# Attention and a gated two-layer MLP on one core: the MLP's layers in stretches of four blocks, Mish and Exp in separate phases, scores in four PSUM banks

## The chip, the core and the metric

The kernel runs on one core of a Trainium2 chip. The metric is the device time of one execution in microseconds. TensorE (PE) multiplies, VectorE (DVE) and ScalarE (ACT) do elementwise work, GpSimd (POOL) does a few fills, SyncE (SP) issues all DMAs. Each engine works through its own list of instructions in order; an instruction that waits for a semaphore holds up everything behind it on its engine.

## The reference, cut to what matters

```python
# q, k, v: (8, 8, 576, 64); f: (8, 8, 576); w_in: (512, 2048); w_out: (2048, 512), float32
scores = q @ k.T / 8 + (cum[:, :, :, None] - cum[:, :, None, :])   # cum = cumsum(log(clip(f)))
scores = where(causal, -1e9, scores)
attn = exp(scores - max(scores)); attn = attn / (sum(attn) + 1e-9)
x = (attn @ v), heads side by side                                 # (4608, 512)
h = x @ w_in
out = (h * tanh(softplus(h))) @ w_out                              # Mish, then the second layer
```

Float32 accuracy is kept by splitting each factor into a high and a low float16 part and adding three products.

## The kernel before, in words

**The work.** Attention goes by pairs of heads: 32 pairs, four to a batch element. The MLP goes by chunks of 512 tokens: eight chunks from the eight batch elements, and a ninth from their last 64 tokens each. A chunk needs the attention output of its four pairs, transposed, in the tile `xa`.

**A pair of heads** (from the fifth pair on; `new_st_items`, L1119). Its scores come in six blocks, X0, Y0, Z, W (with a small V), X1, Y1, each of one PSUM bank. For a block PE makes the scores (`b<-st`), DVE adds the mask and takes the row maximum in one custom instruction (`b<-b,mskw`, with its accumulator read `mn`), ACT takes Exp from PSUM into a float32 buffer (`st<-b,mn`; the buffer is one of two in the tile `flat2`, L1116), ACT copies that to float16 (`hb<-st`), DVE makes the low part (`hb<-st,hb`), and a DMA transposes both into `pt`. Two slots of the order later PE multiplies by v (`new_pv_items`, L1213: 30 products of 64 or 65 columns for the first head, 60 with the tail for the second; `b<-vv,pt`), DVE normalises (`rr`, `x`), and the result is split and transposed into `xa`. For a coming pair ACT sums squares (`junk<-qk`, `junk<-v`), and DVE or ACT scale and split q, k and v (`hl`, `vv`). The first four pairs are done in another way, with float32 products against v.

**A block of the MLP** (16 to a chunk). The first layer (`m1_items`, L1348) is 12 products of 512 columns into bank 2 or 3 in turn (`b<-xa,wall`); ACT takes Mish (`me<-b,cinv`), DVE or ACT the high part `gh`, DVE the low part `gl`. The second layer (`m2_items`, L1380) is 12 products of 512 columns into banks 4 to 7 (`b<-gh,wall`, `b<-gl,wall`), which sum over the 16 blocks and are then copied out as `ot`. Before, the second layer of a block follows the first layer two blocks behind (`LAG` in the main loop, L1503 and on), across chunk boundaries too. In the first chunk the weights are being unpacked and split as well (`wall`).

**Banks.** Scores, products with v and small sums take banks 0 and 1 in turn (`bank`, L883). Banks 2 and 3 belong to the first layer.

**Mish and Exp** are in two different tables of ACT. A change between them puts an `ACT_TABLE_LOAD` ahead of the next one.

**The order.** `Program` records all operations with their regions, and `schedule` (L294) makes the order: forward passes (L355) that take on each engine, at its own clock by a table of costs, the ripe operation of lowest rank, and backward passes that make the next ranks; the best of ten is written out. In the forward pass ACT prefers an operation of the table that is loaded, within the bound `TSWAP` of ranks. The recorded order mixes attention items among MLP items of the chunk before by their costs (last loop of `attn_moe`, L1571 and on).

Of the kernel before, what the change touches and what calls it, by code (L numbers as in the profile page):

```python
# [15 lines left out]
F32 = mybir.dt.float32  # L16
# [10 lines left out]
P = 128  # L27
# [30 lines left out]
WN = [int(x) for x in ("1", "2",)]  # L58
NME = 5
NOT = 2  # L60
NGH = 5
SPD = 0
WO0 = 16
LWO = 4
# [77 lines left out]
class Program:  # L142
# [9 lines left out]
    def __init__(self, nc):  # L152
        self.nc = nc
        self.ops = []
        self.banks = []
        self.sets = []
        self.rank = None
        for n in self.NAMES:
            setattr(self, n, Queue(self, n))

# [3 lines left out]
    def choose(self, *ways):  # L164
# [24 lines left out]
        self.ops.append((opts, r, w, key))  # L189
        func = ways[0][0][3].get("func") if ways[0][0][0] == "scalar" and len(ways) == 1 else None  # L190
        self.sets.append("mish" if func == AF.Mish else "exp" if func == AF.Exp else None)

        self.banks.append({
            x.tensor.name for _, _, a, kw in ways[0] for x in list(a) + list(kw.values())
# [27 lines left out]
    def cost(self, eng, method, kw, aps):  # L222
# [10 lines left out]
        if eng == "tensor":  # L233

            rows = int(kw.get("in_", kw.get("rhs")).shape[0])
            half = (int(out.offset) // int(out.ap[0][0]) // 64 + 1) * (int(out.shape[0]) == 64)
            if kw.get("rhs") is not None and kw["rhs"].dtype == F32:
                n = max(4 * n, 4 * int(out.shape[0]))
            return max(n, 64), n * rows / 128.0, half
        if eng == "scalar":  # L240
            if method != "activation":
                return 1283
# [314 lines left out]
def attn_moe(ctx: ExitStack, tc: tile.TileContext, qk, v, f, w_in, w_out, out):  # L557
# [325 lines left out]
    def bank(name, shape=(P, CH), dtype=F32):  # L883

        nonlocal nbank
        nbank += 1
        return psum(banks[nbank % len(banks)], shape, dtype)

    def load_qk(g):
        b, p = divmod(g, NP)  # L890
        t = sp.tile([P, 2, S], F32, name=f"qk{g}", tag="qk32", bufs=NQK)
        nc.sync.dma_start(out=t, in_=qk[b, p])
        st[g]["qk"] = t
# [220 lines left out]


    flat2 = ST1[2].rearrange("p j t s -> p (j t s)").bitcast(F32)  # L1116
    ne = [0]

    def new_st_items(g):  # L1119
# [20 lines left out]

        def place_e():
            ne[0] += 1
            return flat2[:, CH * (ne[0] % 2) : CH * (ne[0] % 2 + 1)]

        def turn(e, name):
            h = sp.tile([P, 2, CH], F16, name=f"h{name}{g}", tag="hb", bufs=NHB)
# [4 lines left out]
            s[name] = t  # L1151

        def x_(j):
            ps = bank(f"sx{j}_{g}")
            scores(ps, j, 3 * P, P, 0, CH)
            highest(ps, 4 * j + 3, mskw)
            e = place_e()
            exp(e, ps, 4 * j + 3)
            turn(e, f"X{j}")

        def y_(j):
            ps = bank(f"sy{j}_{g}")
            scores(ps[:, 0:384], j, 2 * P, P, 0, 384)
            scores(ps[:, 384:512], j, 0, P, 0, P)
            highest(ps[:, 0:384], 4 * j + 2, mskw[:, 128:512])
            highest(ps[:, 384:512], 4 * j, mskb)
            e = place_e()
            exp(e[:, 0:384], ps[:, 0:384], 4 * j + 2)
            exp(e[:, 384:512], ps[:, 384:512], 4 * j)
            turn(e, f"Y{j}")  # L1170

        def z_():
            ps = bank(f"sz_{g}")
            for j in range(2):
                scores(ps[:, 256 * j : 256 * j + 256], j, P, P, 0, 256)
            for j in range(2):
                highest(ps[:, 256 * j : 256 * j + 256], 4 * j + 1, mskw[:, 256:512])
            e = place_e()
            for j in range(2):
                w = slice(256 * j, 256 * j + 256)  # L1180
                exp(e[:, w], ps[:, w], 4 * j + 1)
            turn(e, "Z")

        def w_():
            ps, pv = bank(f"sw_{g}"), bank(f"sv_{g}")
            for o, k in ((pv[:, 0:D], slice(CH, S)), (ps, slice(0, CH))):
                beside(*((
                    o[j * D : (j + 1) * D], q1[0 : KM - 1, j, CH:S], k1[0 : KM - 1, j, k], True, False)
# [311 lines left out]
    def w0(fn):  # L1500
        M.append((fn, 0))

    LAG = 2  # L1503
    steps = [(c, j) for c in range(NCHUNK) for j in range(NF)]
    done = 0
    i = 0
    while done < len(steps):
        if i < len(steps):
            c, j = steps[i]
            if j == 0:  # L1510
                cstart[c] = len(M)
                if c == 1:
                    w0(level_all)
                if c:
                    w0(lambda c=c: scale_chunk2(c))
                if c == B:
                    for b in range(B):
                        w0(lambda b=b: scale_tails(b))
            items = m1_items(c, j)
        else:  # L1520
            items = []
        M.extend(items)
        lag = LAG0 if done < NF else LAG
        n = 0
        while i - done >= lag and n < 2 and done < len(steps):
            x = m2_items(*steps[done])
            M.extend(x)
            done += 1
            n += 1
            if i - done < LAG:  # L1530
                break
        i += 1

    ai = 0

# [35 lines left out]
    for c in range(NCHUNK):  # L1571
# [3 lines left out]
        target = marks[last_pair(c + 1)] if c + 1 < NCHUNK else len(A)  # L1575
        a_from = ai
        acost = sum(60 + x[1] for x in A[a_from:target])
        mcost = sum(x[1] for x in M[m0:m1])
        done_a = done_m = 0.0
        for k in range(m0, m1):  # L1580
            M[k][0]()
            done_m += M[k][1]
            while ai < target and done_a < acost * (done_m / mcost):
                done_a += 60 + A[ai][1]
                run_a(ai + 1)
        run_a(target)
    nc.emit()


# [48 lines left out]
```

## Time and profile before

| | |
|---|---|
| time, three runs | 1054.42 us median (1052.96 to 1054.48) |
| the profiled execution | 1054.26 us, span 1052.5 us |
| mean granted TensorE clock | 0.984 |
| busy, of the span | PE 94%, ACT 74%, DVE 70%, POOL 2% |
| table loads on ACT | 202 and one at the start, 1283 ns each |
| bytes | 48.37 MB read, 12.57 MB written in HBM |

The page of the profile gives busy time by engine, the span in 40 slices, the chain of waits that ended last, and groups of instructions. All recorded operations have line L290, the line that writes them out, so groups are told apart by tile names. A busy time is that of the instructions' spans, which overlap; PE's ends are modelled.

### The profile page before, as it was taken

Reading aid. Unit: us, or ns where it says so; the run is one execution under the profiler, and the core shown is the slowest. Engines: PE = TensorE matmul, PEld = TensorE weight load, DVE = VectorE, ACT = ScalarE, POOL = GpSimd, SP = SyncE. Lnnn points to the kernel's source line nnn. Section 1 sums busy time; section 2 is a strip of 40 time slices with the busy share of each in tenths; the row PEclk is TensorE's granted clock in tenths of the full one; section 3 lists DMA queues with packets and bytes.
Section 4 is the critical chain, followed back from the end, with each engine's and each line's share of the span. In section 5 each row is a group of like instructions: output and inputs, shape, how many; then the busy total and the mean of one; then the engine's idle time right before and its main releaser. Section 6 shows DMA issues by size and latency. Waiting matters only on the chain.

```text
span 1052.5 us, 19788 instructions
## 1 busy us (share of the span) xinstructions
PE 987.3 (94%) x7214; PEld 504.9 (48%) x7214; DVE 733.5 (70%) x2040; ACT 779.1 (74%) x1293; POOL 17.3 (2%) x59
## 2 busy tenths in 40 slices
PE   0599788999999999999999999999999999999998
PEld 0387344544445555554544554455544554444443
DVE  8989899998677787777777767787777653222221
ACT  5457899879799999898889989899989782112111
POOL 5000000000000000000000000000000000000000
PEclk9799988999999999999999999999999999999999
DMA  9888997877756766777566756775656432000001
GB/s 297 282 232 212 219 225 174 184 197 190 167 136 149 173 141 152 136 169 143 135 145 138 162 123 143 170 158 128 139 122 149 66 66 73 1 1 21 21 1 40
DMA packets 266258, 146.80 MB, mean 139 GB/s; under 512 B 233808, under 2 KB 234576, under 8 KB 266160
## 3 DMA queue, kind: packets, MB, share of 16 engines
q1 hardware_dynamic: 266160, 145.54, 59.0%
q8 instruction: 56, 0.92, 0.4%
q14 instruction: 42, 0.34, 0.1%
HBM read 48.37 MB, written 12.57 MB: 58 GB/s over the span
## 4 chain that ended last, share of the span: by engine, by line
PE 65%; DVE 13%; ACT 11%; DMA 7%; issue 3%; SPq 1%; ACTq 0%; DVEq 0%
PE b L290 65%; ACT L290 3%; DMA pt<-hb 3%; DVE b L290 2%; ACT st L290 2%; DVE wall L290 2%; ACT hb L290 2%; DVE hl L290 2%; DVE hb L290 2%; ACT junk L290 1%; DVE gl L290 1%; ACT me L290 1%; DMA wall<-in_w_in_dram 1%; DMA qk<-in_qk_dram 1%; DVE vv L290 1%
## 5 line engine op out<-in xcount | busy, mean ns | idle before, releaser
L290 PEld LDWEIGHTS <-wall 128*128 128x128 f16 x3456 | 331.7, 98 | 399.6 <-issue 22.4
L290 PE MATMUL b<-xa,wall 128*128 128x512 f16 x1728 | 418.1, 382 | 10.3 <-DVE wall L290 4.4
L290 PE MATMUL b<-gh,wall 128*128 128x512 f16 x1152 | 371.8, 380 | 0.1
L290 ACT ACT_TABLE_LOAD x202 | 259.2, 1283 | 6.6 <-DVE mn L290 2.6
L290 PE MATMUL b<-gl,wall 128*128 128x512 f16 x576 | 218.9, 380 | 0.0
L290 ACT ACTIVATE me<-b,cinv 128x512 f32<-128x512 f32 x144 | 98.8, 687 | 139.5 <-PE b L290 138.2
L290 DVE TENSOR_SCALAR gh<-me,gsc 128x512 f16<-128x512 f32 x125 | 60.3, 483 | 143.3 <-ACT me L290 142.6
L290 PE MATMUL b<-st 70*128 70x256 f16 (+11 forms) x888 | 139.0, 295 | 21.9 <-ACT st L290 5.2
L290 DVE TENSOR_TENSOR hb<-st,hb 128x512 f16<-128x512 f32 x168 | 114.3, 688 | 57.0 <-ACT hb L290 56.9
L290 ACT ACTIVATE st<-b,mn 128x512 f32<-128x512 f32 (+3 forms) x252 | 127.0, 541 | 34.4 <-DVE mn L290 29.6
L290 PE MATMUL b<-vv,pt 128*128 128x65 f16 (+5 forms) x2576 | 105.2, 202 | 5.6 <-ACT st L290 2.5
L290 DVE SCALAR_TENSOR_TENSOR gl<-me,gsc,gh 128x512 f16<-128x512 f32 x144 | 107.9, 750 | 3.5 <-ACT gh L290 0.3
L290 ACT ACTIVATE hb<-st 128x512 f16<-128x512 f32 x168 | 103.5, 628 | 6.6 <-DMA pt<-hb 5.5
L290 PEld LDWEIGHTS <-st 70*128 70x128 f16 (+3 forms) x888 | 67.6, 104 | 83.2 <-issue 46.0
L290 DVE CUSTOM_DVE_ANT_0 b<-b,mskw 128x512 f32<-128x512 f32 (+1 forms) x168 | 93.9, 565 | 17.6 <-PE b L290 15.1
L290 PEld LDWEIGHTS <-pt 128*128 128x128 f16 (+1 forms) x2352 | 72.5, 102 | 24.3 <-DMA pt<-hb 6.8
L290 DVE SCALAR_TENSOR_TENSOR hl<-qk,qt,hl 128x576 f16<-128x576 f32 x64 | 50.8, 810 | 0.7 <-ACT hl L290 0.7
L290 ACT ACTIVATE junk<-qk 128x576 bf16<-128x576 f32 x64 | 43.5, 679 | 5.9 <-DMA qk<-in_qk_dram 5.2
L290 DVE SCALAR_TENSOR_TENSOR wall<-wall 128x512 int32<-128x512 int32 x64 | 43.5, 686 | 0.1
L290 DVE DVE_READ_ACCUMULATOR2_ANT mn<- 128x1 f32 x280 | 39.8, 142 | 0.0
L290 DVE CUSTOM_DVE_ANT_0 b<-b,mskb 128x128 f32<-128x128 f32 (+1 forms) x84 | 23.6, 281 | 18.4 <-PE b L290 13.5
L290 ACT ACTIVATE junk<-wall 128x512 bf16<-128x512 f32 x32 | 20.1, 628 | 18.8 <-issue 10.5
(102 smaller groups left out, 605.2 us busy)
## 6 DMA issues: line engine op xcount, KB each, us to landing
st<-hl SPq DMA_DIRECT2D x192, 144.0 KB
qk<-in_qk_dram SPq DMA_DIRECT2D x32, 576.0 KB
v<-in_v_dram SPq DMA_DIRECT2D x32, 288.0 KB
out_dram<-ot SPq DMA_DIRECT2D x36, 256.0 KB
wall<-in_w_in_dram SPq DMA_DIRECT2D x16, 512.0 KB
wall<-in_w_out_dram SPq DMA_DIRECT2D x16, 512.0 KB
pt<-hb SPq DMA_TRANSPOSE x168
part<-ot SPq DMA_DIRECT2D x8, 256.0 KB
```

What stands on the lines that cost most here:

```text
L290: r = getattr(real[eng], method)(*a, **kw)
```

## The change

- **Stretches.** From the second chunk on the MLP no longer runs with the second layer two blocks behind: the first layer of four blocks is recorded, then the second layer of these four (`GJ = 4`), four such stretches to a chunk, with nothing of one chunk over into the next. The first chunk is as before.
- **Phases.** Each first-layer part and each second-layer part of a stretch is a phase with a number. Every Mish and every Exp recorded in a phase is made to depend on all Mish and Exp of the phase before. Attention items are now mixed in only among second-layer items, so that Exp falls into second-layer phases and Mish into first-layer phases.
- **Banks.** In the phases scores take banks 0 to 3 in turn (`score_bank`); products with v stay in banks 0 and 1, the first layer in 2 and 3.
- **Buffers.** Two more float32 buffers for Exp (`more_e`, four in all), six `gh`/`gl` pairs instead of five. The scratch space of the DMA rings is set smaller; no instruction uses it.
- **Costs in the order.** A float32 product against v counts 4 times its columns, not at least 512, and half as much activity.

```diff
-NGH = 5
+NGH = 6
+GJ = 4
+NEX = 2
...
+        if self.sets[-1] and self.phase is not None:
+            n = len(self.sets)
+            w.append((f"phase{self.phase}", 0, 1, n, n + 1))
+            r.append((f"phase{self.phase - 1}", 0, 1, 0, 1 << 30))
...
             if kw.get("rhs") is not None and kw["rhs"].dtype == F32:
-                n = max(4 * n, 4 * int(out.shape[0]))
-            return max(n, 64), n * rows / 128.0, half
+                n, active = 4 * n, 2 * active
+            return max(n, 64), active, half
...
+    def score_bank(name):
+        nonlocal nbank
+        if nc.phase is None:
+            return bank(name)
+        nbank += 1
+        return psum(nbank % 4)
...
-            return flat2[:, CH * (ne[0] % 2) : CH * (ne[0] % 2 + 1)]
+            k = ne[0] % (2 + NEX)
+            if k > 1:
+                return more_e[:, k - 2]
+            return flat2[:, CH * k : CH * (k + 1)]
...
-            ps = bank(f"sx{j}_{g}")
+            ps = score_bank(f"sx{j}_{g}")
...
+        for j0 in range(0, NF, GJ):
+            for items in (m1_items, m2_items):
+                phases += 1
+                for j in range(j0, j0 + GJ):
+                    M.extend(x + (phases,) for x in items(c, j))
...
-        mcost = sum(x[1] for x in M[m0:m1])
+        weigh = [x[1] * (len(x) < 3 or x[2] % 2 == 0) for x in M[m0:m1]]
+        mcost = sum(weigh)
         for k in range(m0, m1):
+            nc.phase = M[k][2] if len(M[k]) > 2 else None
             M[k][0]()
-            done_m += M[k][1]
+            done_m += weigh[k - m0]
```

In the program that comes out ACT has 69 table loads instead of 203, and 995 rows instead of 1106; PE's 7214 products are the same. Up to the 16th Mish, the last of the first chunk, the loads are 19 and were 21. Of the operations that either ACT or DVE may do, ACT now has 30 `gh` (19 before) and 40 `xp` (23 before).

**ACT, third chunk.** First before, around its ninth block. `me` is the result of Mish, `st1`, `e4` that of Exp, `hb` and `hv` their float16 copies, `b0` to `b7` are PSUM banks:

```order
L290 ACT_TABLE_LOAD
L290 ACTIVATE me_0_167<-b2_0_117,cinv3_96 128x512
L290 ACT_TABLE_LOAD
L290 ACTIVATE st1_2_84<-b1_0_115,mn_1_166 128x512
L290 ACTIVATE st1_2_84<-b0_0_124,mn_1_166 128x384
L290 ACTIVATE hb_0_162<-st1_2_84 128x512
L290 ACTIVATE st1_2_84<-b0_0_124,mn_1_166 128x128
L290 ACTIVATE xa2_89<-xb_0_183 64x2x64
L290 ACTIVATE hb_1_163<-st1_2_84 128x512
L290 ACTIVATE xa2_89<-xb_0_183 64x2x64
L290 ACT_TABLE_LOAD
L290 ACTIVATE me_1_170<-b3_0_118,cinv3_96 128x512
```

Now, around the Mish of the 13th to 16th block:

```order
L298 ACTIVATE hb_1_164<-more_e_102 128x512
L298 ACT_TABLE_LOAD
L298 ACTIVATE me_4_180<-b2_0_118,cinv3_96 128x512
L298 ACTIVATE hb_0_163<-more_e_102 128x512
L298 ACTIVATE me_0_168<-b3_0_119,cinv3_96 128x512
L298 ACTIVATE gh_3_178<-me_0_168,gsc3_100 128x512
L298 ACTIVATE hb_1_164<-st1_2_84 128x512
L298 ACTIVATE me_1_171<-b2_0_118,cinv3_96 128x512
L298 ACTIVATE hl_0_109<-qk32_0_104,qt_2_135 128x576
L298 ACTIVATE me_2_174<-b3_0_119,cinv3_96 128x512
L298 ACT_TABLE_LOAD
L298 ACTIVATE st1_2_84<-b1_0_116,mn_0_162 128x512
```

One Mish between two loads has become four; the float16 copies of the last scores stand among them.

**PE, third chunk.** Before, where a block's first layer (bank 3, `xa`) runs among second-layer products (`gh`, `gl`) and scores (`st1`, `st2`):

```order
L290 MATMUL b7_0_127<-gh_2_174,wall_69 128x512
L290 LDWEIGHTS wall_69
L290 MATMUL b3_0_118<-xa0_87,wall_69 128x512
L290 LDWEIGHTS st1_0_82
L290 MATMUL b0_0_124<-st1_0_82 128x256
L290 LDWEIGHTS st2_1_86
L290 MATMUL b0_0_124<-st2_1_86 128x256
L290 LDWEIGHTS st1_0_82
L290 MATMUL b0_0_124<-st1_0_82 128x256
L290 LDWEIGHTS st2_1_86
L290 MATMUL b0_0_124<-st2_1_86 128x256
L290 LDWEIGHTS wall_69
```

Now, from the last second-layer products of a stretch to the first product of the next stretch. The six second-layer products ahead of these rows follow on the two products of block X1, which stand in bank 2:

```order
L298 MATMUL b7_0_128<-gh_1_172,wall_69 128x512
L298 LDWEIGHTS st1_0_82
L298 MATMUL b3_0_119<-st1_0_82 128x384
L298 LDWEIGHTS st2_1_86
L298 MATMUL b3_0_119<-st2_1_86 128x384
L298 LDWEIGHTS st1_0_82
L298 MATMUL b3_0_119<-st1_0_82 128x128
L298 LDWEIGHTS st2_1_86
L298 MATMUL b3_0_119<-st2_1_86 128x128
L298 LDWEIGHTS st1_1_83
L298 MATMUL b1_0_116<-st1_1_83 128x512
L298 LDWEIGHTS st2_0_85
```

Block Y1 now stands in bank 3 and X0 of the next pair in bank 1; the next rows are X0's second product and the first layer in bank 2. Before, no score ever stood in bank 2 or 3 while the MLP ran; now each change from second to first layer takes over banks that scores have held.

**DVE at the same place.** Before, a maximum (`ISA`, with the accumulator read as a second row) stands among the parts of Mish:

```order
L290 TENSOR_TENSOR hb_0_162<-st1_2_84,hb_0_162 128x512
L290 ISA b1_0_115,mn_1_166<-b1_0_115,mskb2_80 128x64
L290 ISA mn_1_166 128x1
L290 ISA b0_0_124,mn_1_166<-b0_0_124,mskw_79,mn_1_166 128x512
L290 ISA mn_1_166 128x1
L290 TENSOR_SCALAR gh_1_171<-me_1_170,gsc3_100 128x512
L290 SCALAR_TENSOR_TENSOR gl_1_172<-me_1_170,gsc3_100,gh_1_171 128x512
```

Now, W (bank 0), X1 (bank 2) and Y1 (bank 3) of the same pair:

```order
L298 ISA b0_0_125,mn_2_189<-b0_0_125,mskw_79,mn_2_189 128x512
L298 ISA mn_2_189 128x1
L298 TENSOR_TENSOR hb_1_164<-st1_2_84,hb_1_164 128x512
L298 ISA b2_0_118,mn_2_189<-b2_0_118,mskw_79 128x512
L298 ISA mn_2_189 128x1
L298 TENSOR_TENSOR hb_0_163<-st1_2_84,hb_0_163 128x512
L298 TENSOR_TENSOR hv_0_165<-e4_1_146,hv_0_165 128x128
L298 ISA b3_0_119,mn_2_189<-b3_0_119,mskw_79 128x384
L298 ISA mn_2_189 128x1
```

The maxima of a pair now stand in one run without `gh` and `gl` between them, with low parts of the earlier blocks (`hb`) among them.

**How the 21 changes from second to first layer look**, from the first chunk's end to the end of the regular part (five chunks): in 6 the first layer begins in the bank that X1 held, as above; in 5 the bank of Y1 is wanted about as soon, behind 5 to 11 first-layer products in the other bank; in 10 the bank that is wanted first held W or V, which PE wrote two blocks earlier. The last four stretches with attention are irregular, and from there on the two chunks that are left have no attention.

More of the change, by code (lines that the diff above doesn't have):

```diff
@@ L157, in __init__ @@
         self.rank = None
+        self.phase = None
         for n in self.NAMES:
@@ L236, in cost @@
             half = (int(out.offset) // int(out.ap[0][0]) // 64 + 1) * (int(out.shape[0]) == 64)
+            active = n * rows / 128.0
             if kw.get("rhs") is not None and kw["rhs"].dtype == F32:
-                n = max(4 * n, 4 * int(out.shape[0]))
-            return max(n, 64), n * rows / 128.0, half
+                n, active = 4 * n, 2 * active
+            return max(n, 64), active, half
         if eng == "scalar":
@@ L1116, in attn_moe @@
     flat2 = ST1[2].rearrange("p j t s -> p (j t s)").bitcast(F32)
+    more_e = cp.tile([P, NEX, CH], F32, name="more_e")
     ne = [0]
@@ L1161, in y_ @@
         def y_(j):
-            ps = bank(f"sy{j}_{g}")
+            ps = score_bank(f"sy{j}_{g}")
             scores(ps[:, 0:384], j, 2 * P, P, 0, 384)
@@ L1172, in z_ @@
         def z_():
-            ps = bank(f"sz_{g}")
+            ps = score_bank(f"sz_{g}")
             for j in range(2):
@@ L1184, in w_ @@
         def w_():
-            ps, pv = bank(f"sw_{g}"), bank(f"sv_{g}")
+            ps, pv = score_bank(f"sw_{g}"), score_bank(f"sv_{g}")
             for o, k in ((pv[:, 0:D], slice(CH, S)), (ps, slice(0, CH))):
@@ L1503, in attn_moe @@
     LAG = 2
[L1504 to L1532, printed above, removed]
+    phases = 0
+    for c in range(NCHUNK):
+        cstart[c] = len(M)
+        if c == 1:
+            w0(level_all)
+        if c:
+            w0(lambda c=c: scale_chunk2(c))
+        if c == B:
+            for b in range(B):
+                w0(lambda b=b: scale_tails(b))
+        if c == 0:
+            done = i = 0
+            while done < NF:
+                if i < NF:
+                    M.extend(m1_items(c, i))
+                n = 0
+                while i - done >= LAG0 and n < 2 and done < NF:
+                    M.extend(m2_items(c, done))
+                    done += 1
+                    n += 1
+                    if i - done < LAG:
+                        break
+                i += 1
+            continue
+        for j0 in range(0, NF, GJ):
[3 more added lines that the diff above has]
+                    M.extend(x + (phases,) for x in items(c, j))
     ai = 0
@@ L1586, in attn_moe @@
         run_a(target)
+    nc.phase = None
     nc.emit()
@@ L1621 @@
     from concourse.bass_utils import run_bass_kernel_spmd
-    nc = bacc.Bacc("TRN2", target_bir_lowering=False, num_devices=1)
+    nc = bacc.Bacc("TRN2", target_bir_lowering=False, num_devices=1, dynamic_dma_scratch_size=1024)
     data = _layout(inputs)
```

## The prediction, made before the changed kernel ran

> **What bounds the kernel now.** First the page: busy time by engine and the slices of the span, each slice 26.3 us.
>
> ```profile
> PE 987.3 (94%) x7214; PEld 504.9 (48%) x7214; DVE 733.5 (70%) x2040; ACT 779.1 (74%) x1293; POOL 17.3 (2%) x59
> ...
> PE   0599788999999999999999999999999999999998
> ...
> DVE  8989899998677787777777767787777653222221
> ACT  5457899879799999898889989899989782112111
> ...
> PEclk9799988999999999999999999999999999999999
> ```
>
> ACT is nearly as full as PE until slice 33 and then falls idle, while PE stays full; DVE is full only in the first ten slices. A share over the whole span says little, so next the windows, cut where the stages change: attention of the first batch, first chunk with the weights unpacked, four windows of the steady part, and the MLP alone.
>
> ```profile
> core 0: us, PE busy (x) PEld busy (x) DVE busy (x) ACT busy (x) POOL busy (x), PEclk, DMA share, GB/s
> 0.00:97.00 97.00, 60.86 (x545) 48.27 (x545) 85.58 (x232) 53.99 (x124) 13.61 (x32) 0.93 0.87 254
> 97.00:240.00 143.00, 125.87 (x923) 62.19 (x923) 137.34 (x410) 126.86 (x235) 0.69 (x5) 0.93 0.90 205
> 240.00:400.00 160.00, 155.91 (x1214) 77.66 (x1213) 121.64 (x358) 144.61 (x236) 0.83 (x6) 1.00 0.68 158
> 400.00:560.00 160.00, 159.02 (x1259) 80.61 (x1258) 119.30 (x337) 142.92 (x226) 0.83 (x6) 1.00 0.66 145
> 560.00:720.00 160.00, 157.15 (x1244) 79.53 (x1245) 121.28 (x353) 146.86 (x231) 0.83 (x6) 1.00 0.66 148
> 720.00:875.00 155.00, 154.76 (x1234) 78.07 (x1233) 105.68 (x283) 131.83 (x199) 0.55 (x4) 1.00 0.52 110
> 875.00:1050.00 175.00, 173.68 (x805) 78.56 (x803) 42.69 (x73) 32.02 (x49) 0.00 (x0) 1.00 0.06 19
> ```
>
> Here is the whole question. From 875 us on PE does nothing but products of 512 columns, at 173.68/805 = 0.216 us each, without gaps. From 240 to 875 us it idles 4.09 + 0.98 + 2.85 + 0.24 = 8.2 us of 635, though ACT is busy 566 us of them. So PE sets the time there and ACT follows. From 97 to 240 us PE idles 17.1 us, and there DVE, with 137.3 of 143 us, is the fullest. Since the change leaves PE's products as they are, 8.2 us is all that the steady part can give, whatever ACT is spared, and 143 - 137.3 = 5.7 us is about all that the first chunk can give as long as DVE has the same work. What PE waits for in the steady part, by the waits of PE from 240 to 875 us:
>
> ```profile
> PE b L290 <- ACT st L290: 1.8, 5, 0.6
> PE b L290 <- DVE x L290: 1.8, 2, 1.4
> PE b L290 <- ACT me L290: 1.3, 1, 1.3
> PE b L290 <- ACT e L290: 1.1, 1, 1.1
> ```
>
> Columns are the sum in us, the times and the longest. These are four small releases by ACT and DVE and no regular wait: the staggered order of before hides almost everything.
>
> **The change, part by part.** *Table loads.* The groups of ACT from 240 to 875 us, and below them the loads from 97 to 240 us:
>
> ```profile
> L290 ACT ACT_TABLE_LOAD x178 | 228.4, 1283 | 5.9 <-DVE mn L290 2.3 <-DVE rr L290 0.5
> L290 ACT ACTIVATE hb<-st 128x512 f16<-128x512 f32 x138 | 84.9, 628 | 3.4 <-DMA pt<-hb 2.5
> ...
> L290 ACT ACTIVATE st<-b,mn 128x512 f32<-128x512 f32 x69 | 47.2, 685 | 1.0 <-DVE mn L290 0.5
> ```
>
> ```profile
> L290 ACT ACT_TABLE_LOAD x24 | 30.8, 1283 | 1.2 <-DVE rr L290 0.5 <-DVE mn L290 0.3
> ```
>
> The program now has 69 loads, 19 of them by the 16th Mish; 134 fewer at 1.283 us are 172 us of ACT, nearly all behind 240 us. ACT without loads is 566 - 228 = 338 us there; with some 50 loads (64 us) it would be about 402 of 635, 63% instead of 89%. None of the 172 us lies on the path that sets the end, because PE does not wait for them now: this part is worth only what it takes from the 8.2 us. Three of the four waits above are for ACT, and DVE's `x` is late where ACT's copies are; I take 7 of the 8.2 us as gone, with 3 and 8.2 as bounds. [...]
>
> ```profile
> 506.06 0.69 ACT L290 ACTIVATE me<-b,cinv 128x512 f32<-128x512 f32 x1
> 506.76 1.28 ACT L290 ACT_TABLE_LOAD   x1
> ```
>
> The load starts 0.01 us after Mish ends, so the trace shows no drain ahead of it, and I use 1.283.
>
> *Four blocks ahead.* The first layer of four blocks is 48 products, 48 x 0.216 = 10.4 us; the second layer as much, with a pair's attention among it. Within the first layer a block needs its bank back from the Mish two blocks earlier, 2.6 us after that block's end; Mish takes 0.69 us. The second layer begins with a block whose Mish lay 7 us back, and its fourth block comes over 7 us after the last Mish. The six `gh`/`gl` pairs cover that, so this costs nothing as long as the first Mish of a stretch is not over 1.5 us late; then the third block would wait for the excess.
>
> *Banks handed from scores to the first layer.* This is the wait that the change adds, and the term that decides. At the 21 regular changes a first-layer block takes a bank that a score block has just held. It waits for DVE's maximum and ACT's Exp of that block; behind it on PE's queue stands everything, since PE takes products in order. The shortest such chain is in the timeline, from a score block's last product to its maximum:
>
> ```profile
> 510.46 0.60 PE L290 MATMUL b<-st 70*128 70x512 f16 x2
> ...
> 511.09 0.70 DVE L290 CUSTOM_DVE_ANT_0 b<-b,mskw 128x512 f32<-128x512 f32 x1
> ...
> 511.71 0.14 DVE L290 DVE_READ_ACCUMULATOR2_ANT mn<- 128x1 f32 x1
> 511.71 0.33 DVE L290 CUSTOM_DVE_ANT_0 b<-b,mskb 128x128 f32<-128x128 f32 x1
> ```
>
> The products end at 511.06, the maximum is there at 511.85, and Exp takes 0.685: 1.5 us. In the 6 changes of the first kind the block X1 is followed by 6 second-layer products (1.30 us), Y1 (two products each of 384 and 128 columns, 0.43 us) and mostly X0 (0.43 us), about 2.2 us. With free engines nothing waits. But DVE has W's maximum and a low part ahead of X1's, and ACT has a copy and V's Exp:
>
> ```profile
> L290 DVE TENSOR_TENSOR hb<-st,hb 128x512 f16<-128x512 f32 x138 | 94.0, 688 | 53.6 <-ACT hb L290 53.6
> ...
> L290 DVE CUSTOM_DVE_ANT_0 b<-b,mskw,mn 128x512 f32<-128x512 f32 x23 | 17.4, 758 | 0.7
> ```
>
> If these two (0.69 + 0.76 us) and one ACT copy (0.63) all stood in the way, the chain would be 1.5 + 2.1 = 3.6 us and the wait 1.4. DVE's instructions overlap (511.09 to 511.71 is 0.62 for one of 0.70), and W's maximum begins 1.7 us before X1 is there, so most of it is over by then. I take 0.4 us, nearer the lower end. In the 5 changes of the second kind Y1's bank is wanted 5 to 11 products (1.1 to 2.4 us) after its last product, and its chain is a maximum of 128 columns (0.33 + 0.14), Exp of two parts, and the queue: 0 to 1.4 us, taken as 0.7. In the 10 others the bank was written by W or V some 3.5 us before, with W's Exp behind W's maximum: 0 to 0.8, taken as 0. Sum: 6 x 0.4 + 5 x 0.7 = 5.9 us, between 0 and 6 x 1.4 + 5 x 1.4 + 10 x 0.8 = 23 us. A wait of one stretch is not made good in the next, because PE has no idle time to give back. The four irregular stretches I count at nothing.
>
> *First chunk.* It has no phases. The order there moves by the other count of float32 products, the two new Exp buffers and the sixth `gh`: DVE's work up to the end of the chunk is the same to an instruction or two, with two loads fewer on ACT. I take 1.5 us of gain, bounds a loss of 3 and a gain of 5.7. The last two chunks, without attention, are full now and stay so.
>
> **The sum**, against the profiled execution's own 1054.26 us (1.8 us outside the span of 1052.5, 0.2 us from the median of the runs, 1054.42): 1054.3 - 7.0 - 1.5 + 5.9 = 1051.7 us.
>
> **Rivals.** *All of the idle goes and nothing comes.* If ACT at 63% makes every Exp early, the changes of layers cost nothing, and the first chunk gives all that DVE leaves: 1054.3 - 8.2 - 5.7 = 1040.4 us. For it speaks that three of four waits are ACT's; against it, that DVE's load is as before, and that DVE stands in the same chain.
>
> *DVE is late at the changes of layers.* The mechanism is the one above with its price at the upper side: maxima of a pair now come in one run, DVE reaches X1, Y1 and W a microsecond later than PE wants their banks, and each of the 21 changes costs 1.0 us. That is 21 us; with 7 us gained it gives 1054.3 + 21 - 7 = 1068 us. It decides from a mean wait of (7 + 1.5)/21 = 0.4 us on. For it speaks that DVE's busy share in the second-layer part rises: scores, low parts and normalisation of a pair, most of the 468 us of DVE in the steady windows, now fall into some 15 us of each 26. Against it, that DVE is at 74% there and can catch up while PE does 10.4 us of first layer.
>
> *ACT was never in the way.* The waits of before are accidents of order, as many come back elsewhere, and the changes of layers cost nothing: 1054 us, no difference.
>
> *The clock falls.* From 97 to 240 us PE idles 12% and the granted clock is 0.93. If each change of layers idled PE as much, 535 us at 0.93 would cost 40 us: 1094 us. The slices at full clock from 240 us on, with waits of up to 1.4 us in them, speak against it. [...]
>
> **How the numbers follow.** A measurement of this kernel can tell some 0.2%, 2.1 us, from no change. My forecast has a chance of 0.43, between 1048 and 1056 us: 0.25 of it faster than 1052.3, 0.15 within, 0.03 slower. The rival that gains all has 0.20, all faster; late DVE 0.27, all slower; no difference 0.08, of which 0.07 within and 0.01 slower; the clock 0.02, slower. That makes 0.45 faster, 0.22 same, 0.33 slower. The range reaches to 1041 at the side of the full gain and to 1069 past late DVE; half of the first rival and a fifth of the second lie outside. The likeliest case has 1048 to 1056 for itself.
>
> **What would show it.** Right: about 68 loads on ACT; ACT near 63% busy and PE's idle from 240 us on about 7 us in all, in waits of some 0.4 us for Exp ahead of first-layer products; the end of the first chunk within 3 us of its place. Late DVE would show as waits of 1 us or more of PE for `st` or `me`, once in 26 us. The forecast is wrong if PE's idle time in the steady part is over 15 us or under 2, or if the first chunk's end moves by more than 6 us either way.

## The result and the profile after

The changed kernel takes 1062.28 us (median of four runs, 1059.64 to 1064.08), the kernel before 1054.45 us beside it. The ratio is 1.0072 with a 95% interval of 1.0056 to 1.0088: slower by 0.7%. The profiled execution has a span of 1059.0 us at a mean granted clock of 0.981. First the page's busy times, then the windows, cut where those of before were cut:

```profile
PE 983.6 (93%) x7214; PEld 507.0 (48%) x7214; DVE 725.3 (68%) x2010; ACT 623.3 (59%) x1189; POOL 16.7 (2%) x59
```

```profile
0.00:97.00 97.00, 60.53 (x535) 47.30 (x535) 81.21 (x222) 50.27 (x114) 12.94 (x32) 0.93 0.82 243
97.00:240.00 143.00, 119.56 (x866) 60.69 (x865) 134.72 (x401) 117.47 (x226) 0.69 (x5) 0.90 0.87 200
240.00:400.00 160.00, 158.00 (x1252) 80.45 (x1250) 119.21 (x339) 109.72 (x211) 0.83 (x6) 1.00 0.71 157
400.00:560.00 160.00, 158.01 (x1260) 80.34 (x1258) 118.63 (x336) 106.81 (x205) 0.84 (x6) 1.00 0.68 149
560.00:720.00 160.00, 155.10 (x1197) 78.39 (x1195) 119.83 (x353) 111.89 (x214) 0.70 (x5) 1.00 0.70 154
720.00:875.00 155.00, 154.06 (x1213) 77.93 (x1212) 106.36 (x284) 91.98 (x167) 0.69 (x5) 1.00 0.46 105
875.00:1059.00 184.00, 178.32 (x904) 81.87 (x901) 45.30 (x82) 35.19 (x54) 0.00 (x0) 1.00 0.08 25
```

ACT fell from 74% to 59% of the span, as the loads left it. From 240 to 875 us PE's busy time is much what it was (625.2 us after, 626.8 before). The second row is the one that moved: PE has 866 products from 97 to 240 us, and had 923, its busy time is 6.3 us less and the clock 0.90 instead of 0.93.

Windows at fixed times hold different work in two kernels, so a second ruler is needed. The MLP makes 3456 products with `wall`, 384 to a chunk, all of them in the traces. The start of the n-th of them, counted in each trace:

| product | before, us | after, us | what lies up to it |
|---|---|---|---|
| 144 | 158.7 | 157.4 | |
| 192 | 185.7 | 194.3 | half of the first chunk |
| 384 | 235.9 | 244.2 | the first chunk |
| 2688 | 882.5 | 887.0 | the six chunks with attention beside them |
| 3456 | 1048.3 | 1054.8 | the last two chunks |

The first chunk ends 8.3 us later, and all of that, and more, is lost between products 144 and 192. The next six chunks are 3.8 us shorter (642.8 instead of 646.6), the last two 2.0 us longer. What PE waits for from 97 to 240 us, first before, then after (sum, times, longest):

```profile
PE b L290 <- ACT st L290: 6.4, 8, 1.5
PE b L290 <- DVE wall L290: 4.4, 3, 1.8
PE b L290 <- DMA xa<-xp: 3.0, 1, 3.0
```

```profile
PE b L298 <- ACT st L298: 9.8, 5, 3.5
PE b L298 <- ACT more_e L298: 9.1, 9, 2.8
PE b L298 <- DVE wall L298: 2.0, 1, 2.0
```

The first kernel waits in eight small pieces for Exp, the second in 14, some of them long. And from 240 to 880 us, after:

```profile
PE b L298 <- ACT me L298: 4.1, 4, 2.1
PE b L298 <- ACT st L298: 2.7, 6, 0.5
PE b L298 <- ACT more_e L298: 2.4, 3, 1.3
PE b L298 <- DVE x L298: 0.4, 2, 0.2
```

### The profile page after: what moved, and what is told of

It is laid out like the page before. It is cut to its first block, busy times and chain, and to the rows that moved or that the text cites. A ratio compares the mean times of both kernels' runs of the same rounds, so it can differ in the third digit from the quotient of the medians.

```text
span 1059.0 us, 19555 instructions
## 1 busy us (share of the span) xinstructions
PE 983.6 (93%) x7214; PEld 507.0 (48%) x7214; DVE 725.3 (68%) x2010; ACT 623.3 (59%) x1189; POOL 16.7 (2%) x59
## 4 chain that ended last, share of the span: by engine, by line
PE 59%; DVE 18%; ACT 10%; DMA 7%; issue 4%; SPq 1%; DVEq 0%; ACTq 0%
PE b L298 59%; DVE wall L298 3%; DVE b L298 3%; ACT junk L298 2%; DVE hb L298 2%; DMA qk<-in_qk_dram 2%; DVE hl L298 2%; DMA st<-hl 2%; ACT st L298 2%; DMA pt<-hb 1%; DVE vv L298 1%; ACT hb L298 1%; ACT more_e L298 1%; DVE xp L298 1%; SPq L298 1%
## 5 line engine op out<-in xcount | busy, mean ns | idle before, releaser
L298 PE MATMUL b<-xa,wall 128*128 128x512 f16 x1728 | 390.5, 382 | 14.3 <-ACT me L298 5.9
L298 PE MATMUL b<-st 70*128 70x256 f16 (+12 forms) x888 | 136.3, 296 | 28.6 <-ACT more_e L298 6.6
L298 DVE CUSTOM_DVE_ANT_0 b<-b,mskw 128x256 f32<-128x256 f32 (+2 forms) x168 | 94.9, 565 | 13.7 <-PE b L298 11.8
L298 ACT ACTIVATE more_e<-b,mn 128x512 f32<-128x512 f32 (+3 forms) x126 | 64.4, 544 | 41.5 <-DVE mn L298 38.9
L298 ACT ACTIVATE st<-b,mn 128x512 f32<-128x512 f32 (+3 forms) x126 | 65.1, 544 | 35.7 <-DVE mn L298 30.3
L298 DVE TENSOR_TENSOR hb<-more_e,hb 128x512 f16<-128x512 f32 x84 | 57.3, 686 | 26.7 <-ACT hb L298 26.5
L298 DVE TENSOR_TENSOR hb<-st,hb 128x512 f16<-128x512 f32 x84 | 57.7, 688 | 25.7 <-ACT hb L298 25.5
L298 ACT ACTIVATE hb<-st 128x512 f16<-128x512 f32 x84 | 52.5, 626 | 5.3 <-DMA pt<-hb 4.3
L298 ACT ACTIVATE hb<-more_e 128x512 f16<-128x512 f32 x84 | 52.1, 627 | 3.1 <-DMA pt<-hb 2.7
L298 ACT ACTIVATE xp<-x 128x128 f16<-128x128 f32 (+1 forms) x40 | 15.5, 401 | 50.1 <-DVE x L298 50.1
```

The lines of the kernel that those rows point to most:

```text
L298: r = getattr(real[eng], method)(*a, **kw)
```

## The experiments

The theory after the two traces: the stretches gain as forecast, and the first chunk lost by a new order that the planner made of it. The rivals: the stretches themselves cost the time; or a single edit, the float32 count or the Exp buffers, makes the start worse.

**Which part of the program, by exchanging the starts.** In e1 the changed kernel hands out its first 2301 operations in the order of the kernel before, and everything behind them as the change has it. In e2 the kernel before (with the buffers the order needs) gets the first 2300 operations in the changed order. `FIRST` is a table of operations and engines:

```diff
+FIRST = [
...
+        first = [(x // 4, 0) for x in FIRST]
...
+            for n, (i, _) in enumerate(first):
+                rank[i] = n - 1e9
...
-        return best[1]
+        known = {i for i, _ in first}
+        return first + [x for x in best[1] if x[0] not in known]
```

> The changed kernel, but its first 2301 operations (up to product 384 of the MLP, the end of the first chunk) are handed out in the very order in which the kernel before hands them out; stretches, phases, four score banks, buffers and the new float32 count stay for all that follows. Theory (the loss is the new order of the first chunk, the steady part gains): product 384 starts near 236 us as before, and the time is 1062.3 - 8.3 = 1054.0 us, or lower by the steady part's gain if that holds with this start, 1052 to 1054.5. Rival 1 (the stretches and phases cost the time, and the late first chunk is only a shift): 1060 to 1063 us. Rival 2 (the end of the first chunk is bound by loads of weights and v, not by the order): product 384 stays near 244 us.

> The kernel before (with the two more Exp buffers, the sixth gh pair and the smaller DMA scratch, which the order needs), its first 2300 operations handed out in the order of the changed kernel; everything after the first chunk is in the old manner (no stretches, no phases, two banks). Theory: product 384 starts near 244 us, time 1054.4 + 8.3 = 1062.7 us (1061 to 1064). Rival 1 (stretches and phases cost the time): 1053 to 1056 us.

| | rest as before | rest as changed |
|---|---|---|
| start as before | 1054.2 | e1: 1051.3 (ratio to before 0.9974, interval 0.9964 to 0.9984) |
| start as changed | e2: 1066.2 (1.0119, 1.0106 to 1.0132) | the changed kernel: 1062.3 |

The four times nearly add: the new start costs 11 to 12 us, whatever follows; the new rest gains 3 to 4 us, whatever went ahead. Product 384 starts at 234.6 us in e1 and at 247.2 in e2. The windows from 97 to 240 us of e1 and of e2 look like those of before and of after:

```profile
97.00:240.00 143.00, 125.27 (x895) 61.01 (x895) 137.61 (x408) 128.02 (x239) 0.69 (x5) 0.94 0.92 206
```

```profile
97.00:240.00 143.00, 118.60 (x852) 59.40 (x852) 132.82 (x394) 114.59 (x220) 0.69 (x5) 0.89 0.87 196
```

So the stretches and phases did gain; the loss is the order of the first chunk, whose code the change hardly touches. Rival 1 of these runs fell. Both times lie a little outside the ranges expected, e1 below (1052 to 1054.5), e2 above (1061 to 1064). The intervals cover the spread of executions, not that of orders that the planner may make; the table of all starts below shows how wide that is.

**What re-made that order.** Three edits reach into the first chunk: the count, the Exp buffers and the sixth `gh` pair (not tried by itself, but e3 keeps it). e3 undoes the float32 count, e4 keeps the two more Exp buffers out of it:

```diff
-                n, active = 4 * n, 2 * active
-            return max(n, 64), active, half
+                n = max(4 * n, 4 * int(out.shape[0]))
+            return max(n, 64), n * rows / 128.0, half
```

```diff
-            k = ne[0] % (2 + NEX)
+            k = ne[0] % (2 + (NEX if nc.phase is not None else 0))
```

> The changed kernel with the old column count of float32 products. Rival A (the new count alone made the start worse): product 384 near 236 us and 1053 to 1055 us. Theory (any edit re-makes the order of the first chunk, and this one was an unlucky draw): the order of the first chunk is a third one, product 384 anywhere from 234 to 246 us and the time that much off: 1052 to 1064, with the part after product 384 within 2 us of the changed kernel's 810.6 us.

> The changed kernel, but the two more Exp buffers are used only behind the first chunk. Rival B (four Exp buffers in the first chunk let ACT run ahead with Exp and keep the products of PE waiting): product 384 near 236 us, 1053 to 1055 us. Theory (unlucky draw of the order): a third order, product 384 anywhere from 234 to 246 us, 1052 to 1064 us, the part after it within 2 us of 810.6.

e3 takes 1047.1 us (0.9930, 0.9918 to 0.9942) with product 384 at 232.9; e4 takes 1060.4 (1.0063, 1.0050 to 1.0077) with 245.7. e3 is better than either of its expectations had it, and in both the part behind product 384 is shorter than expected (806.9 and 807.7 us). As the sole cause the buffers are out, and so is the sixth `gh` pair, since e3 has both and starts early. But any edit gives another order of the first chunk, and one early start may be luck. So draws were made with each count: the ranks at the outset get a random amount below 1 ns, nothing else.

```diff
-SEED = 122
-NZ = 0
+SEED = 1
+NZ = 1
```

> The changed kernel with ranks that differ at the outset by a random amount below 1 ns (nothing else differs): another draw of the order of the first chunk. Theory (luck of the draw): product 384 lands anywhere between 233 and 246 us, and the time follows it as 810 + product 384 + 8: 1051 to 1064. Rival A (the new float32 count makes every start bad): product 384 at 243 to 248 us, 1060 to 1066.

> As the draw before, with other random numbers. Theory: product 384 anywhere between 233 and 246 us; that this, the first draw and the changed kernel all lie above 242 has a chance of about one in eight if good and bad starts are equally likely. Rival A: above 242 again.

> The changed kernel with the old float32 count and a random amount below 1 ns on the ranks. Theory (luck): product 384 anywhere between 233 and 246 us. Rival A (the count decides): 232 to 236 us, 1046 to 1050 us.

> As the draw before, with other random numbers. Theory (luck): anywhere between 233 and 246 us, and the two counts' draws overlap. Rival A: 232 to 236 us, and no draw with the old count is as late as any with the new.

The new count gave 1060.2 and 1073.0 us, the old 1054.5 and 1054.3. With the new count product 384 starts at 245.1 and 257.5 us, the second later than luck was to allow; with the old at 241.8 and 240.7, which is what luck said and later than rival A. Luck is worth several us, but the counts do not overlap. Next the new count alone in the kernel before (g1), and the two halves of the edit, columns and activity, apart in the changed kernel (g2, g3):

```diff
-                n, active = 4 * n, 2 * active
+                n, active = 4 * n, max(4 * n, 4 * int(out.shape[0])) * rows / 128.0   # g2
+                n, active = max(4 * n, 4 * int(out.shape[0])), 2 * active             # g3
```

> The kernel before with nothing but the new float32 count. So far the four starts drawn with the new count put product 384 at 244 to 258 us, the three with the old count and the kernel before at 233 to 242. Rival A in its new form (the new count shifts the starts by some 10 us, whatever follows): product 384 at 242 to 252 us and 1060 to 1068 us. Luck alone: 233 to 246 us, 1051 to 1064.

> The changed kernel with half of the count undone: float32 products cost four columns each as in the change, but enter the planner's reckoning of the clock with the old, larger activity. If the larger activity is what made the old starts good (the planner reckons with the full clock while the float32 products run, as the trace shows it): product 384 at 233 to 242 us. If the column count did it: 244 to 258 us. Luck: anything, 233 to 258.

> The other half undone: old column count (at least 512 for a product with 128 rows out), new activity. If the columns did it: product 384 at 233 to 242 us; if the activity did it: 244 to 258 us.

g1 takes 1065.2 us (1.0110, 1.0091 to 1.0130): that one line costs the kernel before 11 us. g2 takes 1060.0, with product 384 at 242.3 us between its two ranges; g3 takes 1046.0 (0.9931, 0.9918 to 0.9945), with 227.6, earlier than either of its own. The columns do it, not the activity. And of the columns, those of the wide products (65 columns, the first pairs' probabilities times v) or of the narrow ones (1 to 6, sums over rows):

```diff
+                n, active = max(4 * n, 4 * int(out.shape[0]) * (n > 32)), 2 * active    # k1
+                n, active = max(4 * n, 4 * int(out.shape[0]) * (n <= 32)), 2 * active   # k2
+                n, active = 4 * n * (4 if n > 32 else 1), 2 * active                    # k4
```

> The changed kernel; only the wide float32 products (65 columns: the probabilities times v of the first pairs) get the old, larger count of 512 columns, the narrow ones keep the new. Theory C (the larger count of the wide products makes the planner put more of VectorE's weight conversions ahead of the instruction that reads such a product's bank, so that VectorE, in order, does not stand still): VectorE busy 39 to 43 us of the stretch 50 to 97 us as in all orders made with the old count (34.5 to 36.5 in all with the new), product 384 at 228 to 242 us, 1046 to 1055 us. If the narrow products matter instead: 35 to 36 us and 242 to 257, over 1060.

> The reverse: only the narrow float32 products (1 to 6 columns: sums and largest values over the rows) get the old count of 512, the wide ones keep the new. Theory C: VectorE busy 34 to 37 us of 50 to 97 us, product 384 at 242 to 257 us, 1059 to 1070 us. If the narrow ones matter: 39 to 43 us, 228 to 242 us, 1046 to 1055 us.

> The changed kernel with sixteen columns for each of a wide float32 product (1040 for 65, twice the old count), the narrow ones as in the change. Theory C (the count acts as a margin): VectorE busy 39 us or more of 50 to 97 us, product 384 below 242 us, 1044 to 1056 us. If only a count near the old 512 suits: the start is as late as with the new, over 242 us.

k1 takes 1049.1 us (0.9952, 0.9937 to 0.9967), k2 1065.3 (1.0108, 1.0093 to 1.0123): it is the wide ones. k4 takes 1084.6: with twice the old count the start is worse than any other, so the count is no mere margin of which more is better, and theory C's forecast for k4 failed.

**Which engine is the bound in the late starts.** All orders with the new count have less work of DVE from 50 to 97 us, where the wide products run. Before, then after:

```profile
50.00:97.00 47.00, 46.96 (x460) 39.69 (x458) 40.98 (x122) 29.35 (x67) 0.36 (x3) 1.00 0.84 218
```

```profile
50.00:97.00 47.00, 45.26 (x445) 38.16 (x443) 35.70 (x107) 24.74 (x55) 0.37 (x3) 1.00 0.70 185
```

DVE is busy for 41.0 and 35.7 us; over all orders made by the planner it is 39.0 to 43.2 with the old count and 34.2 to 36.5 with the new. By 97 us DVE has started 62 conversions into `wall` before and 55 after; 60 to 72 in the six orders of the planner with 512 columns for a wide product, 54 to 57 in the seven with 260. In k3 the changed order is kept, but 14 conversions of weights on DVE are moved ahead of the six instructions at which DVE stood still. In l1 ten conversions between 100 and 190 us are left out (6.8 us of DVE's instructions, which overlap: its busy time up to product 384 falls from 219.9 to 215.7 us), in l2 17 sums of squares are cut short (6.8 us of ACT), with no change to the order of the start:

```diff
             for eng, method, a, kw in ops[i][0][o][1]:
+                if i in LEAVE:                                                     # l1
+                    continue
+                if i in CUT:                                                       # l2
+                    kw = dict(kw, out=kw["out"][:, 0:32], in_=kw["in_"][:, 0:32])
```

> The changed kernel with the new count and its own order of the first chunk, in which 14 weight conversions of VectorE are moved ahead of the six instructions before which VectorE stood still for 1.0 to 3.2 us each between 50 and 98 us (10.8 us in all; the conversions take about 8 us); PE's and ScalarE's orders are as they were. Theory C, in its narrowest form (that idle time of VectorE is what is missing later, when conversions stand ahead of the maxima): VectorE busy 40 to 44 us of 50 to 97 us, product 384 at 236 to 240 us instead of 244.2, time 1054 to 1058. If the idle time of VectorE there is only a companion of another cause in the order of PE or ScalarE: product 384 within 2 us of 244.2, 1060 to 1063.

> The changed kernel in its own order of the first chunk, with ten of VectorE's weight conversions left out between 100 and 190 us (the third step of ten of them, which sets the last three bits of the mantissa; 10 x 0.68 = 6.8 us). Theory D (in the late starts VectorE has too much left to do behind 97 us, and the products wait for maxima that stand behind conversions on it): product 384 is 4 to 8 us earlier than 244.2, 236 to 240, with more than half of it before product 192. If VectorE is only busy beside a bound on ScalarE: less than 2 us.

> The changed kernel in its own order of the first chunk, with 17 of ScalarE's sums of squares of weights between 100 and 190 us taken over 32 of 512 columns, so that their scales are off (17 x 0.4 = 6.8 us of ScalarE, as much as the other kernel takes from VectorE). Theory D: less than 3 us, product 384 at 241 to 244. If ScalarE's queue is the bound there (it is what the waits of PE name): 4 to 8 us earlier, 236 to 240.

None of the three starts earlier: k3 takes 1062.1 us, l1 1061.3, l2 1059.8, with product 384 at 247.0, 246.5 and 244.8 (changed kernel: 244.2). So the gain that C expected of k3, D of l1, and D's rival of l2 did not come. By l1 and l2 neither the amount of work on DVE nor that on ACT, taken alone, bounds the late start, and theory D is wrong. C in its narrow form was hardly put to the test: in k3 DVE reached only 37.5 us in the window, where 40 to 44 were meant, since it then stood still at other places.

**What the traces then show: the loads of the weights.** A load of weights overwrites a staging slot that conversions must have emptied, and it stands in SP's queue among the transposes: the last one after the change waits 3.0 us there for a conversion. The rows of these loads in the traces of before, of after and of k1 (first and last start at the end):

```profile
L290 SPq DMA_DIRECT2D wall<-in_w_out_dram x16: 332/430/576, 21.3 to 172.9; - x16
```

```profile
L298 SPq DMA_DIRECT2D wall<-in_w_out_dram x16: 346/426/583, 20.7 to 188.3; - x16
```

```profile
L298 SPq DMA_DIRECT2D wall<-in_w_out_dram x16: 327/381/536, 20.4 to 165.9; - x16
```

The last load is issued 15 us later after the change. All starts, where "order of" means a replayed order:

| kernel | columns of a wide product | last load, us | product 384, us | from there to product 3456, us | median time, us |
|---|---|---|---|---|---|
| g3 | 512 | 163 | 227.6 | 814.0 | 1046.0 |
| k1 | 512 | 166 | 231.4 | 811.7 | 1049.1 |
| g4 | 512, order of before | 170 | 232.5 | 822.1 | 1063.9 |
| e1 | 512, order of before | 172 | 234.6 | 810.7 | 1051.3 |
| e3 | 512 | 172 | 232.9 | 806.9 | 1047.1 |
| before | 512 | 173 | 235.9 | 812.4 | 1054.4 |
| f4 | 512 | 173 | 240.7 | 809.4 | 1054.3 |
| f3 | 512 | 186 | 241.8 | 810.6 | 1054.5 |
| g1 | 260 | 179 | 246.4 | 812.2 | 1065.2 |
| e4 | 260 | 187 | 245.7 | 807.7 | 1060.4 |
| after | 260 | 188 | 244.2 | 810.6 | 1062.3 |
| f1 | 260 | 188 | 245.1 | 812.2 | 1060.2 |
| g2 | 260 | 188 | 242.3 | 811.7 | 1060.0 |
| l2 | 260, order of after | 189 | 244.8 | 809.6 | 1059.8 |
| e2 | 260, order of after | 190 | 247.2 | 814.9 | 1066.2 |
| l1 | 260, order of after | 190 | 246.5 | 809.3 | 1061.3 |
| k3 | 260, order of after | 191 | 247.0 | 809.8 | 1062.1 |
| k2 | 260 | 193 | 251.0 | 808.7 | 1065.3 |
| f2 | 260 | 203 | 257.5 | 813.4 | 1073.0 |
| k4 | 1040 | 116 | 258.8 | 817.4 | 1084.6 |

(The columns in the middle are from one profiled execution each, which can lie up to 4 us from the median.) Leaving replays and k4 aside, six orders with 512 columns reach product 384 at 227.6 to 241.8 us, seven with 260 at 242.3 to 257.5, without overlap. Product 384 follows the last load by 54 to 68 us in all of the first 19, a spread that is wider than the 8.3 us in question. The part behind product 384 takes 812.2 to 814.9 us in the three kernels with the old rest (before, g1, e2) and 806.9 to 817.4 in the 16 with the changed rest and four banks, so the gain of the new rest, 3 to 4 us by the exchange, hangs on the draw too. How a late load reaches PE is in the timeline of after, between products 144 and 192; a row ends with the wait ahead of it and who ended it:

```profile
180.12 0.52 SPq L298 DMA_DIRECT2D wall<-in_w_out_dram  x1
...
185.28 0.43 DVE L298 TENSOR_SCALAR wall<-wall 128x512 int32<-128x512 int32 x1 [0.92 <-DMA wall<-in_w_out_dram]
...
185.62 0.74 DVE L298 SCALAR_TENSOR_TENSOR gl<-me,gsc,gh 128x512 f16<-128x512 f32 x1
...
186.42 0.59 PE L298 MATMUL b<-gl,wall 128*128 128x512 f16 x1 [1.17 <-DVE gl L298]
```

The load issued at 180.12 lands 5.07 us later; DVE, in order, stands 0.92 us before a conversion of what it brings, behind that stands `gl`, and PE waits 1.17 us for `gl`. The chain of waits that ended last has this load and the one ahead of it after the change (start, us, what):

```profile
173.19 5.83 DMA wall<-in_w_out_dram
...
180.12 5.07 DMA wall<-in_w_out_dram
```

That is 10.9 of the 36.9 us between products 144 and 192. Before, these products are 27.0 us apart and no load stands on the chain between them. But this does not hold for late starts in general. Of the replays of this order e2 and l1 have 10.7 and 10.2 us of loads on the chain there, l2 5.4, and k3 none, with 13.4 us of the transposes `pt` in their place. The late starts of e4, f1, f2, g1, g2 and k2 have 0.1 us at most, while the early ones of e3 and k1 have 6.5 and 4.4. In k3, l1 and l2 the last load stayed at 189 to 191 us, which fits with their late starts and proves nothing. k4 is the other end: its last load goes out at 116 us, but DVE has started 90 conversions by 97 us, and the first MLP product starts at 147.9 us instead of 102.0. So late loads go along with late starts; that they cause them is not shown, and the chains of the other late starts speak against one common cause. No kernel moved the loads alone.

**What the four score banks are worth.** g4 is e1 with scores left in banks 0 and 1 throughout:

```diff
-        nbank += 1
-        return psum(nbank % 4)
+        return bank(name)
```

> The changed kernel with the order of the kernel before up to product 384, and with the scores of the later chunks in the two banks of before instead of all four. If the two more banks carry a gain (products of PE waiting less for ACT's Exp): the part behind product 384 is 2 to 8 us longer than the 810.7 us with four banks, 1053 to 1059 us. If the hand-over of banks at the layer changes costs what the forecast put on it (5.9 us): shorter, 805 us, 1045.5 us. If neither matters: 1050 to 1053.

g4 takes 1063.9 us against e1's 1051.3. Up to product 384 they are alike (232.5 and 234.6 us), the part behind it is 822.1 instead of 810.7. PE's busy time from 240 to 875 us, first e1, then g4, shows only part of this, for it leaves 10.31 us idle in e1 and 13.45 in g4:

```profile
240.00:875.00 635.00, 624.69 (x4951) 317.49 (x4950) 460.43 (x1300) 413.58 (x781) 3.06 (x22) 1.00 0.62 140
```

```profile
240.00:875.00 635.00, 621.55 (x4859) 315.54 (x4858) 458.25 (x1280) 411.90 (x778) 3.05 (x22) 1.00 0.62 138
```

Measured from the start of one product to the start of the next, less 0.42 ns for each of its columns (0.216 us for 512; a product of one column counts as 64, 0.027 us, and the shortest step behind one in the traces of before and after is 0.028), the time lost in pieces over 0.1 us between products 384 and 2688 is 29.0 us in 114 pieces in g4, 16.7 in 49 in e1, 16.1 in 49 after and 19.9 in 98 before. With ACT and DVE as busy as in e1, stretches with two banks would be 9.7 us worse than the staggered order (822.1 against 812.4); the two more banks bring 11.4 us back, more than the 2 to 8 expected. The gain of the rest is theirs, by this one draw: 822.1 lies outside the 806.9 to 817.4 us of the draws with four banks. In g4 no first-layer product waits for Exp from 240 to 880 us; 23 others do, for 7.2 us, 0.5 at most.

## Why the prediction was wrong, point by point

- **The failed step** is "First chunk": "I take 1.5 us of gain, bounds a loss of 3 and a gain of 5.7". The term measured a loss of 8.3 us in the profiled executions, 11 by the exchange of starts (1062.3 - 1051.3). The bound was drawn from the amount of DVE's work, "the same to an instruction or two". The amount was the same (218.8 us of DVE up to product 384 before, 219.9 after), and in l1, with 215.7, product 384 came no earlier: an order was changed, and its price was not in the busy times. The forecast's own sign of being wrong, the first chunk's end off by more than 6 us, came true. The runs put the loss on the order of the first chunk, and the order on the column count of the wide float32 products; which wait inside a late start costs the time stays open. The text named the float32 count as one of three things that move the order and gave it no price. It should have asked where its products stand: this row, of the first pair's product with v, says that 26 of them run in 3.02 us, 0.11 us apart. A product of 512 columns takes 0.216 us, so 4 x 65 columns would be 0.110:

```profile
50.74 3.02 PE L298 MATMUL b<-vv,pt 128*128 128x65 f32 x26
```

- The new count is the truer one; 224 of these products lie between 50 and 98 us of the trace, where the planner chooses between attention and the unpacking of weights. With the old count, nearly twice too long, it unpacked more by 97 us (62 conversions, and 55 after). The planner's best of ten is best by its own costs, and a truer cost of one kind of product gave later starts here: all seven with it are behind all six without.
- **Table loads**: right. This group of ACT from 240 to 875 us (count, busy time, mean ns) was forecast as some 50; ACT is busy 420 of 635 us, 66% (forecast 63%). ACT's busy time there fell by 146 us and the kernel's time behind product 384 by 1.8.

```profile
L298 ACT ACT_TABLE_LOAD x48 | 61.6, 1283 | 0.9
```

- **Banks handed over**: right in kind and size. PE waits 5.1 us in nine pieces for Exp behind 240 us (2.7 and 2.4 in the rows above). Eight of them, 4.8 us, stand ahead of first-layer products at changes of layers; before, none did. The forecast put 5.9 us on eleven changes. Late DVE, the rival, would have been 21 waits of 1 us; of these nine the longest is 1.3.
- **Four blocks ahead**, which "costs nothing as long as the first Mish of a stretch is not over 1.5 us late; then the third block would wait for the excess", was put at nothing and wasn't. The mechanism was named rightly, and the condition failed. PE waits 4.1 us in four pieces for Mish from 240 to 880 us, and before 1.3 in one. All four, and the wait of 1.9 us behind them, stand ahead of the first product of the third block in a chunk's first stretch. In the longest, ACT first writes out sums of the chunk before (`ot`) and loads its table:

```profile
679.81 0.69 ACT L298 ACTIVATE ot<-b,cols 128x512 f32<-128x512 f32 x1 [2.12 <-DMA out_dram<-ot]
...
680.51 1.28 ACT L298 ACT_TABLE_LOAD   x1
681.81 1.27 ACT L298 ACTIVATE me<-b,cinv 128x512 f32<-128x512 f32 x2
...
682.55 1.67 PE L298 MATMUL b<-xa,wall 128*128 128x512 f16 x7 [2.11 <-ACT me L298]
```

- **Steady part**: forecast -7.0 + 5.9 = -1.1 us, measured -3.8 between products 384 and 2688. The ceiling was wrong: 8.2 us of idle time is what the busy time leaves, and from start to start PE lost 19.9 us between these products. The four waits shown in the forecast are not all of that view either: three more, for DVE's `cols` and two DMAs, make 1.5 us. PE idles 9.8 us by the windows after, within the limits that the forecast gave itself, and still the stretch is shorter.
- **Last two chunks**, "full now and stay so": 2.0 us longer. It is one wait for Mish, 1.9 us up to 894.47, at the third block of the first of these chunks (2.1 us from start to start); before, PE loses no piece over 0.1 us there.
- With the old start the change takes 1051.3 us (e1), where the forecast said 1051.7. That is near, but in part luck: 1.5 us of the forecast's gain was for a first chunk whose order e1 does not change. The stretches, forecast at 1.1 us of gain, gained 3 to 4 by the exchange.
- **The clock**: from 97 to 240 us the granted clock was 0.90 instead of 0.93. Three windows of 5 us after the change, around PE's wait of 3.49 us up to 169.72:

```profile
165.00:170.00 5.00, 1.16 (x11) 0.57 (x8) 5.00 (x16) 4.86 (x14) 0.00 (x0) 0.92 0.51 105
170.00:175.00 5.00, 2.40 (x22) 1.45 (x21) 4.48 (x18) 4.90 (x13) 0.00 (x0) 0.50 0.80 193
175.00:180.00 5.00, 5.00 (x31) 2.38 (x29) 4.77 (x17) 4.14 (x11) 0.00 (x0) 0.56 1.15 185
```

PE is busy 1.16 us of the first, and the clock is 0.50 and 0.56 in the two behind it: products of 512 columns that start between 177 and 179 us follow each other 0.43 us apart instead of 0.216, so a second loss came behind the wait. A clock of 0.50 came behind shorter waits too: before the change it is there from 165.9 to 169.2 us, and of the 4 us from 162 to 166 PE was busy 1.93, with no wait over 1.50. From which wait on the clock falls, the runs do not show. From 240 us on it stays at 1.00 in all windows after the change, in g4 too, with its 114 pieces, so the small waits there did not lower it; but in k1 the window from 560 to 720 us has 0.99.

## What to carry to other kernels

When a planner makes the order, an edit of a cost is an edit of the whole program: list the operations that have this cost, find where they stand, and draw several orders, since here one draw differed from the next by up to 13 us. Separate the parts by replaying the order of one kernel's beginning in the other; four times then tell which part gained and which lost. The best kernels of this study, g3 with 1046.0 us and e3 with 1047.1, are the change with the old, less true column count; two more draws of it (f3 and f4) took 1054.5 and 1054.3, no faster than the kernel before, so part of this is a lucky draw.

## What the runs showed of the hardware that was not expected

- Leaving out ten instructions of an engine that is busy 134.7 of 143 us (l1, DVE, 4.2 us of its busy time up to product 384) moved the time by less than 1 us, and cutting short 6.8 us of ACT's (l2) by 2.5 us. Being 94% busy did not make DVE the bound of this stretch.
- A float32 product of 65 columns has a mean duration of 0.28 us in the trace of after (192 of them), but the next follows 0.11 us later; the shown duration is not what it costs on PE.
